# A decode-attention kernel: K loaded for four batches at once, and the engines' loops by fours of batches

## The chip, the cores and the metric

The kernel runs on one core of a Trainium2 chip. The metric is the device time of one execution in microseconds (us). Times below are medians. The profile is of one execution of each kernel. Its span, from the first to the last instruction, is about 1.7 to 2.1 us shorter than the time of the run (194.7 us for 196.53 before the change). Engines: PE is the matmul engine (PEld are its weight loads), DVE the vector engine, ACT the scalar engine, POOL the GpSimd engine, SP the sync engine, which here only issues DMAs.

## The reference

One query token per batch, grouped-query attention over the last 512 keys of a cache, with projections before and after:

```python
B, Sq, D = 32, 1, 512
Hq, Hkv, Sk, Dh = 32, 8, 2048, 128          # all bf16
W = min(4096, max(256, Sk // 4))            # 512
q = (x @ wq).reshape(B, Sq, Hq, Dh).transpose(0, 2, 1, 3)
k = repeat(k_cache[:, :, Sk - W:, :], 4, axis=1)
v = repeat(v_cache[:, :, Sk - W:, :], 4, axis=1)
p = softmax(einsum("bhqd,bhkd->bhqk", q, k) * Dh ** -0.5)
o = einsum("bhqk,bhkd->bhqd", p, v)
return o.transpose(0, 2, 1, 3).reshape(B, Sq, Hq * Dh) @ wo
```

The windows of K and V are 33.5 MB each, wq and wo 4 MB each: 75.5 MB to read, whatever the schedule.

## The kernel before

Per batch, K arrives in two DMAs of 512 KB with 4 KB rows (partition = key block and head). PE transposes it into PSUM, 32 transposes of 128x128 in four banks `KT_ps`. DVE copies three of the banks to `KT_sb`, ACT the fourth. Eight score matmuls per batch accumulate four batches in one PSUM tile `S_ps`. Softmax (maximum on DVE, exponential on ACT, four scaled writes into the block-diagonal `P_ex` on DVE), the transposes of P and their copies on ACT then go by four batches. PV goes by batch, and its result is copied out by DVE (`oT`).

The loops of the three engines are interleaved by batch:

```python
# SP: K runs LEAD = 5 batches ahead of V; rings of NK = 6 and NV = 8 batches
for b in range(B + LEAD):
    if b < B: load_k(b)
    if b >= LEAD: load_v(b - LEAD)
# PE, PVLAG = 6
for it in range(B + PVLAG):
    if it < B: transposes(it)
    if 1 <= it <= B: scores(it - 1)
    if it >= PVLAG: pv_matmuls(it - PVLAG)
    if it % 4 == 1 and 5 <= it <= B + 1: pt_transposes((it - 5) // 4)
    ...                                     # cut: selection of outputs, once, near the end
# DVE
for it in range(B + PVLAG + 1):
    if it < B: kt_evac(it, 0)
    if it >= PVLAG + 1: ot_evac(it - PVLAG - 1)
    ...                                     # cut
    if it % 4 == 1 and 5 <= it <= B + 1: softmax_b((it - 5) // 4)
    if it < B: kt_evac(it, 1); kt_evac(it, 2)
    if it % 4 == 0 and 4 <= it <= B: softmax_a((it - 4) // 4)
# softmax_b, the P_ex write: P_ex is [P, NR=16, NS=32, G4=4]
P_ex[rows, :, :, c], P_f32[rows, :].rearrange("p (r s) -> p r s", r=NR)
# the score operand: KT_sb is [P, NKT=3, 2, NR, G4, NS]
rhs = KT_sb[:, b % NKT, h, :, c, :]         # 16 runs of 32 elements
```

## Time and profile before

| | before |
|---|---|
| time | 196.4 us (3 runs, 196.2 to 196.75) |
| span of the profile | 194.7 us |
| PE, DVE, ACT busy | 74%, 52%, 30% of the span |
| DMA | 16 engines busy in nearly every slice, 405 to 412 GB/s in slices 4 to 38 |

The span of the kernel before in 40 equal slices; digits are tenths (9 is 90% or more), PEclk is the granted clock of PE, GB/s what the DMA engines moved:

```profile
PE   0448995877897679749777988779776978937881
...
PEclk9999999999699978996999699979998887975558
DMA  5999999999999999999999999999999999999960
GB/s 204 426 420 406 412 405 411 407 410 407 409 407 407 408 408 410 407 407 410 407 407 410 409 407 407 410 406 408 408 406 411 405 410 405 412 405 412 406 251 31
```

The DMA row is full from slice 2 to slice 38, and no other row is. The chain of waits that ended last, by engine and then by line (SPq is the DMA queue of SP; L144 issues V, L136 K), says the same:

```profile
SPq 68%; DMA 23%; PE 5%; issue 3%; DVEq 0%; DVE 0%
SPq L144 37%; SPq L136 26%; DMA K_sb<-in_k_cache_dram 15%; DMA w_sb<-in_wo_dram 8%; SPq L155 5%; PE KT_ps L243 4%; SPq L130 1%; PE S_ps L260 1%; PE QO_ps L293 0%; PE KT_ps L337 0%; SPq L118 0%; DVEq L47 0%; DVE out_sb L418 0%
```

The costliest groups (line, engine, operation, output and inputs, count, busy us and mean ns of one, then the idle time before them and its main cause):

```profile
L243 PE MATMUL KT_ps<-perm,K_sb 128*128 128x128 bf16 x1024 | 75.2, 235 | 22.4 <-DMA K_sb<-in_k_cache_dram 22.2
L361 DVE COPY KT_sb<-KT_ps 128x1024 bf16<-128x1024 bf16 x96 | 63.6, 689 | 52.2 <-PE KT_ps L243 52.0
...
L435 ACT ACTIVATE KT_sb<-KT_ps 128x1024 bf16<-128x1024 bf16 x32 | 32.8, 1023 | 82.3 <-PE KT_ps L243 82.3
...
L383 DVE TENSOR_SCALAR P_ex<-P_f,recip 32x512 bf16<-32x512 f32 x32 | 25.4, 793 | 1.2
L260 PE MATMUL S_ps<-KT_sb,QBD 128*32 128x512 bf16 x256 | 22.2, 428 | 0.0
```

And PE's wait for K (total us, times, longest):

```profile
PE KT_ps L243 <- DMA K_sb<-in_k_cache_dram: 22.2, 35, 1.3
```

PE waits for K 35 times, 22 us in all. So it has slack: with faster loads it could go faster. That slack is about 0.7 us (22.2 over 32 batches) in each 5.1 us.

### The profile page before, as it was taken

The numbers are of one execution on the slowest core, as the hardware profiler recorded it, in microseconds if no ns is written. First come the engines' busy times: TensorE is split into PE (matmuls) and PEld (weight loads), VectorE is DVE, ScalarE is ACT, GpSimd is POOL, SyncE is SP. The second block draws the span as 40 slices with busy tenths as digits, with TensorE's granted clock in tenths as the row PEclk, the third lists the DMA queues.
The fourth block names the chain that finished last, engine by engine and source line by source line (L and its number), as shares of the span: only waits on it lengthen the run. The fifth ranks groups of instructions, "written<-read, shape, count | busy, mean of one in ns | idle before, by whom it ended". The sixth has DMA issues, their size and how long they took to land.

```text
span 194.7 us, 6153 instructions
## 1 busy us (share of the span) xinstructions
PE 144.0 (74%) x2724; PEld 114.9 (59%) x2724; DVE 102.1 (52%) x190; ACT 57.6 (30%) x70; POOL 15.0 (8%) x45
## 2 busy tenths in 40 slices
PE   0448995877897679749777988779776978937881
PEld 0337773755586567537555667557666667636760
DVE  0005778745684459533944587447943574670211
ACT  3001535622262126213252236204420352213101
POOL 8502000000020001000000000000000000000000
PEclk9999999999699978996999699979998887975558
DMA  5999999999999999999999999999999999999960
GB/s 204 426 420 406 412 405 411 407 410 407 409 407 407 408 408 410 407 407 410 407 407 410 409 407 407 410 406 408 408 406 411 405 410 405 412 405 412 406 251 31
DMA packets 20282, 75.97 MB, mean 390 GB/s; under 512 B 2272, under 2 KB 2336, under 8 KB 19744
## 3 DMA queue, kind: packets, MB, share of 16 engines
q1 hardware_dynamic: 20208, 75.54, 97.2%
q8 instruction: 22, 0.36, 0.8%
q10 hardware_dynamic: 48, 0.03, 0.1%
q14 instruction: 4, 0.03, 0.0%
HBM read 75.53 MB, written 0.03 MB: 388 GB/s over the span
## 4 chain that ended last, share of the span: by engine, by line
SPq 68%; DMA 23%; PE 5%; issue 3%; DVEq 0%; DVE 0%
SPq L144 37%; SPq L136 26%; DMA K_sb<-in_k_cache_dram 15%; DMA w_sb<-in_wo_dram 8%; SPq L155 5%; PE KT_ps L243 4%; SPq L130 1%; PE S_ps L260 1%; PE QO_ps L293 0%; PE KT_ps L337 0%; SPq L118 0%; DVEq L47 0%; DVE out_sb L418 0%
## 5 line engine op out<-in xcount | busy, mean ns | idle before, releaser
L243 PE MATMUL KT_ps<-perm,K_sb 128*128 128x128 bf16 x1024 | 75.2, 235 | 22.4 <-DMA K_sb<-in_k_cache_dram 22.2
L361 DVE COPY KT_sb<-KT_ps 128x1024 bf16<-128x1024 bf16 x96 | 63.6, 689 | 52.2 <-PE KT_ps L243 52.0
L243 PEld LDWEIGHTS KT_ps<-perm,K_sb 128*128 128x128 bf16 x1024 | 65.6, 106 | 30.0 <-DMA K_sb<-in_k_cache_dram 28.4
L435 ACT ACTIVATE KT_sb<-KT_ps 128x1024 bf16<-128x1024 bf16 x32 | 32.8, 1023 | 82.3 <-PE KT_ps L243 82.3
L293 PEld LDWEIGHTS QO_ps<-PT_sb,V_sb 128*128 128x128 bf16 x1024 | 28.3, 97 | 17.8 <-issue 13.5
L293 PE MATMUL QO_ps<-PT_sb,V_sb 128*128 128x16 bf16 x1024 | 31.1, 171 | 3.3 <-DMA V_sb<-in_v_cache_dram 1.3
L383 DVE TENSOR_SCALAR P_ex<-P_f,recip 32x512 bf16<-32x512 f32 x32 | 25.4, 793 | 1.2
L260 PE MATMUL S_ps<-KT_sb,QBD 128*32 128x512 bf16 x256 | 22.2, 428 | 0.0
L453 ACT ACTIVATE PT_sb<-PT_ps 128x1024 bf16<-128x1024 bf16 x16 | 15.5, 1021 | 19.4 <-PE PT_ps L275 19.4
L203 POOL COPY QBD<-QT_sb 128x32 bf16<-128x32 bf16 x32 | 8.5, 279 | 116.1 <-PE S_ps L260 108.1
L275 PE MATMUL PT_ps<-ident,P_ex 128*128 128x128 bf16 x128 | 9.4, 231 | 9.8 <-DVE P_ex L383 9.8
L275 PEld LDWEIGHTS PT_ps<-ident,P_ex 128*128 128x128 bf16 x128 | 7.9, 104 | 10.9 <-DVE P_ex L383 10.8
L397 DVE CAST oT_sb<-QO_ps 128x32 bf16<-128x32 f32 x32 | 9.3, 289 | 7.5 <-PE QO_ps L293 7.5
L221 PE MATMUL PT_ps<-xT_sb,w_sb 128*128 128x32 bf16 x128 | 4.1, 188 | 6.4 <-DMA w_sb<-in_wq_dram 6.4
L367 DVE TENSOR_REDUCE maxv<-S_ps 128x1 f32<-128x512 f32 x8 | 5.5, 691 | 5.4 <-PE S_ps L260 5.4
L221 PEld LDWEIGHTS PT_ps<-xT_sb,w_sb 128*128 128x128 bf16 x128 | 3.7, 104 | 6.8 <-DMA w_sb<-in_wq_dram 4.6
L443 ACT ACTIVATE P_f<-S_ps,negmax 128x512 f32<-128x512 f32 x8 | 5.5, 687 | 6.3 <-DVE negmax L369 6.3
L260 PEld LDWEIGHTS S_ps<-KT_sb,QBD 128*32 128x32 bf16 x256 | 3.9, 96 | 3.9 <-issue 1.4
L353 DVE CAST QT_sb<-PT_ps 128x512 bf16<-128x512 f32 x1 | 0.7, 691 | 10.3 <-PE PT_ps L221 10.3
L337 PE MATMUL KT_ps<-w_sb,o_sel 128*32 128x128 bf16 x128 | 3.8, 289 | 1.9 <-DMA w_sb<-in_wo_dram 1.5
L337 PEld LDWEIGHTS KT_ps<-w_sb,o_sel 128*32 128x32 bf16 x128 | 2.9, 131 | 2.7 <-DMA w_sb<-in_wo_dram 2.2
L427 ACT ACTIVATE QT_sb<-PT_ps 128x512 bf16<-128x512 f32 x1 | 0.6, 597 | 12.0 <-PE PT_ps L221 12.0
(28 smaller groups left out, 22.4 us busy)
## 6 DMA issues: line engine op xcount, KB each, us to landing
K_sb<-in_k_cache_dram SPq DMA_DIRECT2D x64, 512.0 KB, 15.6
V_sb<-in_v_cache_dram SPq DMA_DIRECT2D x64, 512.0 KB, 15.4
w_sb<-in_wq_dram SPq DMA_DIRECT2D x4, 1024.0 KB, 8.3
w_sb<-in_wo_dram SPq DMA_DIRECT2D x8, 512.0 KB, 15.4
x_sb<-in_x_dram ACTq DMA_DIRECT2D x1, 32.0 KB, 2.9
out_dram<-out_sb SPq DMA_DIRECT2D x1, 32.0 KB, 1.5
```

The source lines that it names most:

```text
L136: sp.dma_start(K_sb[:, b % NK, h].rearrange("p r d -> p (r d)"), cache_rows(k_cache, b, h)).then_inc(sem_k[b % NK][h], 16)
L144: sp.dma_start(V_sb[:, b % NV, h].rearrange("p r d -> p (r d)"), cache_rows(v_cache, b, h)).then_inc(sem_v[b % NV], 16)
L155: sp.dma_start(wo_sb[:, hg].rearrange("p i n -> p (i n)"), wo[hg * 512:(hg + 1) * 512, :].rearrange("(m i) n -> m (i n)", i=4),).then_inc( ...
L243: ins = pe.matmul(KT_ps[:, t, i * 128:(i + 1) * 128], lhsT=K_sb[:, b % NK, h, 8 * (t % 2) + i, :], rhs=perm[:, :, :], start=True, stop=Tru ...
L260: ins = pe.matmul(S_ps[32 * c:32 * c + 32, :], lhsT=QBD[:, b % NQB, g, :], rhs=KT_sb[:, b % NKT, h, :, c, :], start=(j == 0 and h == 0), s ...
L275: ins = pe.matmul(PT_ps[:, r // 8, (r % 8) * 128:(r % 8 + 1) * 128], lhsT=P_ex[:, r, :, :].rearrange("p s g -> p (s g)"), rhs=ident[:, :], ...
L293: ins = pe.matmul(QO_ps[:, 16 * h:16 * h + 16], lhsT=V_sb[:, b % NV, h, r, :], rhs=PT_sb[:, q % 2, r, :].rearrange("p (c n) -> p c n", c=G ...
L361: dve.tensor_copy(KT_sb[:, b % NKT, t // 2, 8 * (t % 2):8 * (t % 2) + 8, :, :], KT_ps[:, t, :]).then_inc(dve_T, 1)
L383: dve.tensor_scalar(P_ex[rows, :, :, c], P_f32[rows, :].rearrange("p (r s) -> p r s", r=NR), recip[rows, q:q + 1], None, op0=ALU.mult,).th ...
L397: dve.tensor_copy(oT_sb[:, :, b], QO_ps[:, 0:HQ]).then_inc(dve_oT, 1)
L435: act.activation(KT_sb[:, b % NKT, 1, 8:16, :, :], KT_ps[:, 3, :], ACTF.Copy).then_inc(act_T, 1)
L453: act.activation(PT_sb[:, q % 2, 8 * i:8 * i + 8, :].rearrange("p r n -> p (r n)"), PT_ps[:, i, :], ACTF.Copy,).then_inc(act_PT, 1)
```

## The change

The intent is longer rows. K's partition becomes (batch, head) x 4 key blocks for four batches at once, so a row is 16 KB and a DMA 2 MB. One transpose now holds 32 (batch, head) pairs, so a score matmul over all 512 keys can start only when all 128 transposes of four batches are copied out. KT becomes one buffer of four batches, and everything goes by fours. Core of the diff:

```diff
-            for b in range(B + LEAD):
-                if b < B:
-                    load_k(b)
-                if b >= LEAD:
-                    load_v(b - LEAD)
+            def load_k(n):                       # 16 chunks of 2 MB, ring of 3
+                q, e = divmod(n, 2)
+                ...
+                rows = k_cache[4*q:4*q+4, :, SK-W:, :].rearrange("b g (s r) d -> (b g) s (r d)", s=KS)
+                sp.dma_start(K_sb[:, n % NK]..., rows[:, :, e*CR*DH:(e+1)*CR*DH])
+            for n in range(NCH):
+                load_k(n)
+                if n >= 2:
+                    load_v(2 * n - 4)
+                    load_v(2 * n - 3)
 ...
-        KT_sb = sb("KT_sb", [P, NKT, 2, NR, G4, NS], BF16)
+        KT_sb = sb("KT_sb", [P, KR, 4 * G, KS], BF16)      # KR = 128, KS = 4
-                        rhs=KT_sb[:, b % NKT, h, :, c, :],
+                            rhs=KT_sb[:, :, G * j + g, :],  # 128 runs of 4 elements
 ...
+            for q in range(NQUAD):               # PE
+                transposes(4 * q)
+                transposes(4 * q + 1)
+                if q >= 1:
+                    pt_transposes(q - 1)
+                    pv_matmuls(4 * q - 4)
+                    pv_matmuls(4 * q - 3)
+                transposes(4 * q + 2)
+                transposes(4 * q + 3)
+                scores(q)                        # 32 matmuls of 512 columns
+                if q >= 1:
+                    pv_matmuls(4 * q - 2)
+                    pv_matmuls(4 * q - 1)
 ...
-                        P_ex[rows, :, :, c], P_f32[rows, :].rearrange("p (r s) -> p r s", r=NR),
+                        P_ex[rows, :, :, c].rearrange("p r (s e) -> p e r s", e=NE),
+                        P_f32[rows, :].rearrange("p (e r s) -> p e r s", e=NE, r=NR),
 ...
+            for q in range(NQUAD):               # DVE
+                kt_evac(4 * q)
+                kt_evac(4 * q + 1)
+                if q >= 1:
+                    ot_evac(4 * q - 4)
+                    ot_evac(4 * q - 3)
+                kt_evac(4 * q + 2)
+                kt_evac(4 * q + 3)
+                softmax_a(q)
+                if q >= 1:
+                    ot_evac(4 * q - 2)
+                    ot_evac(4 * q - 1)
+                softmax_b(q)
```

## The prediction

> **What bounds the kernel now.** DMA. The 40-slice row shows the 16 DMA engines at 90% or more in slices 2 to 38 at 405-412 GB/s; the chain of waits is 68% the sync engine's queue (issues of about 1.08 us each[...]) and 23% DMA. PE is busy 74% of 194.7 us but has slack: its waits on K loads sum to 22.2 us, about 1 us per batch period of 5.1 us.
>
> **What the change does to DMA.** K rows grow from 4 KB to 16 KB. In the trace's packet records a 4 KB packet takes a median 161 ns and an 8 KB one (wq) 309 ns, so about 13 ns are fixed; a 16 KB packet should take about 605 ns instead of 4 x 161. K's 33.5 MB (82 us) should fall by 4 to 5 us; 20.2 thousand packets by about 6 thousand. [...] If DMA still bound, the time would be about 192 us.
>
> **What it does to the schedule.** PE's work is the same, but goes by fours: four batches of transposes, then 32 score matmuls, in one single-buffered KT tile. Overlap between neighbours becomes a serial loop. I walked the wait graph of both kernels with durations of the trace (timeline): 32 transposes 1.97 us, a KT copy 0.65 back to back on DVE and 1.0 on ACT, 8 score matmuls 0.61, maximum 0.69 + 0.15, exponential 0.69 + 0.19, four P_ex writes 3.3, P transposes 1.07, their two copies 1.94, PV 0.96 plus about 0.4 for the oT handshake. The walk of before gives score times within 2 us of the trace.
>
> For after it gives a PE loop of 21.5 us per four batches at full clock, against 19.5 us in which DMA brings four batches. Idle PE per loop: about 3 us while transposes wait for DVE, which must finish P_ex before it drains the next KT banks; 2.5 us in which PV waits for ACT's PT copies; 1.4 us in which scores wait for the last KT copy; 1.1 us oT handshakes. So K waits vanish and PE with its DVE/ACT handshakes becomes critical. First scores about 29.5 us, the eighth about 180, then 22 us of tail (softmax, PT, four PV, selection, output). Span about 204 us at full clock; at the 0.9 granted in the steady slices of before, about 210. The run time is 1.7 us over the span.
>
> The DMA gain is thus off the critical path: loads end earlier or stall on buffers, while PE ends later. A 2 MB first K load also delays the first transposes by about 3 us.
>
> Predicted: 210 us, range 200 to 224; faster 0.06, same 0.08, slower 0.86.
>
> **What would show it.** The chain: PE, DVE and ACT lines instead of the sync queue. Transposes wait on DVE copies rather than on K DMAs. Score start to score start about 21 to 23 us. wo lands well before its matmuls. DMA share falls late; K packets 16 KB near 605 ns.
>
> **What would make it wrong.** (a) The score operand now has 8-byte runs at a 256-byte stride (before 64-byte runs); if PE reads that at half speed, add some 12 us. (b) P_ex writes with stride 64 bytes innermost; if they take 1.1 us instead of 0.8, add about 7. (c) PE idle in lumps may lower the granted clock more. (d) If PE overlaps more than my walk says, DMA stays the bound and the time is 191 to 196. [...]

## The result, and the profile after

The changed kernel takes 248.37 us (4 runs, 247.65 to 249.5), the kernel before 196.33 us beside it. The ratio is 1.2654, 95% interval 1.2613 to 1.2695.

The predicted direction and mechanism show up at once; the size does not. The slices after:

```profile
PE   0418854697278765688269746679269737777365
...
PEclk9999995759975897769975997779875997689755
DMA  6999999999999994799839992998659999700000
```

The DMA row is no longer full, and it ends five slices early. The loads are done by about 216 us of 247. PEclk drops to 5 to 7 tenths in a repeating pattern. The chain is now PE with DVE and ACT (L239 transposes, L387 P_ex writes, L289 PV, L256 scores, L461 copies of the P transposes), and only 7% of it is DMA:

```profile
PE 53%; DVE 22%; ACT 11%; DMA 7%; issue 6%; SPq 1%; DVEq 0%; ACTq 0%
PE KT_ps L239 30%; DVE P_ex L387 14%; PE QO_ps L289 10%; PE S_ps L256 8%; DMA K_sb<-in_k_cache_dram 7%; ACT PT_sb L461 6%; ACT KT_sb L443 4%; DVE oT_sb L402 2%; DVE maxv L371 2%; PE PT_ps L271 2%; DVE KT_sb L365 2%; PE KT_ps L339 1%; DVE recip L379 1%; SPq L131 1%; DVE negmax L373 1%
```

The same groups as before:

```profile
L239 PE MATMUL KT_ps<-ident,K_sb 128*128 128x128 bf16 x1024 | 89.9, 272 | 39.8 <-DVE KT_sb L365 35.2
...
L365 DVE COPY KT_sb<-KT_ps 128x1024 bf16<-128x1024 bf16 x96 | 63.2, 689 | 22.4 <-PE KT_ps L239 22.1
L443 ACT ACTIVATE KT_sb<-KT_ps 128x1024 bf16<-128x1024 bf16 x32 | 32.7, 1023 | 128.9 <-PE KT_ps L239 128.9
...
L387 DVE TENSOR_SCALAR P_ex<-P_f,recip 32x512 bf16<-32x512 f32 x32 | 42.7, 1335 | 1.2
...
L256 PE MATMUL S_ps<-KT_sb,QBD 128*32 128x512 bf16 x256 | 19.7, 451 | 10.4 <-ACT KT_sb L443 10.4
```

The KT copies cost per instruction what they cost before, on DVE (689 ns) and on ACT (1023 ns). Three means have grown: the P_ex write from 793 to 1335 ns, the transposes from 235 to 272 ns, the score matmul from 428 to 451 ns. (The score group as a whole is busy less, 19.7 us in place of 22.2: in the kernel before, six of the 32 bursts of eight fell into stretches of half clock and took 1.02 to 1.04 us in place of 0.61.) PE's waits have changed kind. Two new ones, and the old one, which happens once, at the start:

```profile
PE KT_ps L239 <- DVE KT_sb L365: 35.2, 7, 6.3
...
PE QO_ps L289 <- ACT PT_sb L461: 15.5, 8, 2.1
...
PE KT_ps L239 <- DMA K_sb<-in_k_cache_dram: 4.7, 1, 4.7
```

And SP's own waits show that DMA is no longer in the way. It waits 129 us for K buffers to come free, and at the end 41 us with everything issued:

```profile
SPq L138 <- PE KT_ps L239: 129.1, 13, 17.5
SPq L164 <- ACT out_sb L483: 40.6, 1, 40.6
```

One loop of four batches, in order of time (start us, us, engine, line, operation, tiles, count, and in brackets the idle time before and what ended it):

```profile
111.67 2.47 PE L256 MATMUL S_ps<-KT_sb,QBD 128*32 128x512 bf16 x32 [1.32 <-ACT KT_sb L443]
...
114.06 0.96 PE L289 MATMUL QO_ps<-PT_sb,V_sb 128*128 128x16 bf16 x32
...
116.23 1.95 PE L239 MATMUL KT_ps<-ident,K_sb 128*128 128x128 bf16 x32
...
116.77 5.45 DVE L387 TENSOR_SCALAR P_ex<-P_f,recip 32x512 bf16<-32x512 f32 x4
...
123.00 3.47 PE L239 MATMUL KT_ps<-ident,K_sb 128*128 128x128 bf16 x32 [4.82 <-DVE KT_sb L365]
...
126.31 1.06 PE L271 MATMUL PT_ps<-ident,P_ex 128*128 128x128 bf16 x16
...
127.43 1.94 ACT L461 ACTIVATE PT_sb<-PT_ps 128x1024 bf16<-128x1024 bf16 x2
...
129.42 1.01 PE L289 MATMUL QO_ps<-PT_sb,V_sb 128*128 128x16 bf16 x32 [2.05 <-ACT PT_sb L461]
...
131.69 5.99 PE L239 MATMUL KT_ps<-ident,K_sb 128*128 128x128 bf16 x64
```

The loop is serial. Scores end at 114.1. Softmax runs until 122.2, of which 5.45 us are four P_ex writes. Only then does DVE copy the next KT banks, and PE, which has filled all four banks at 118.2, stands still for 4.8 us. The 32 transposes after it take 3.47 us, and the 64 at 131.69 take 5.99, where the 32 at 116.23 take 1.95. The next scores start at 138.99, 27.3 us after these. PE by stretch in the same loop (length, PE busy and count, granted clock, DMA share, GB/s) shows why:

```profile
118.20:123.00 4.80, 0.00 (x0) 0.98 0.89 359
123.00:126.30 3.30, 3.30 (x32) 0.51 0.02 6
129.40:131.70 2.30, 1.89 (x65) 0.55 0.97 413
131.70:135.20 3.50, 3.50 (x40) 0.50 0.97 404
```

After the idle stretch the granted clock is half, and again from 129.4 to 135. The clock records of this trace are 0.5 or 1.0, in stretches of 3.4, 6.8 or 13.7 us (17.2 us for the last). The half clock from 122.8 us follows the idle 4.8 us, the half clock from 129.6 us an idle stretch of only 2.05 us. From 123.0 to 126.2 us PE ran nothing but transposes, and from 126.2 us the clock was full. How long PE may idle before the clock falls is not shown: in the kernel before, no wait of PE between 40 and 150 us was longer than 1.35 us, and the clock was still at half for 3.4 us about every 20 us (mean 0.91 from 45 to 100 us).

### The profile page after: what moved, and what is told of

It is laid out like the page before. It is cut to its first block, busy times and chain, and to the rows that moved or that the text cites. A ratio compares the mean times of both kernels' runs of the same rounds, so it can differ in the third digit from the quotient of the medians. Undisturbed runs are those within 1.5% of the kernel's fastest.

```text
span 247.1 us, 5986 instructions
## 1 busy us (share of the span) xinstructions
PE 157.0 (64%) x2724; PEld 138.4 (56%) x2724; DVE 124.8 (51%) x190; ACT 56.9 (23%) x70; POOL 11.9 (5%) x43
## 4 chain that ended last, share of the span: by engine, by line
PE 53%; DVE 22%; ACT 11%; DMA 7%; issue 6%; SPq 1%; DVEq 0%; ACTq 0%
PE KT_ps L239 30%; DVE P_ex L387 14%; PE QO_ps L289 10%; PE S_ps L256 8%; DMA K_sb<-in_k_cache_dram 7%; ACT PT_sb L461 6%; ACT KT_sb L443 4%; DVE oT_sb L402 2%; DVE maxv L371 2%; PE PT_ps L271 2%; DVE KT_sb L365 2%; PE KT_ps L339 1%; DVE recip L379 1%; SPq L131 1%; DVE negmax L373 1%
## 5 line engine op out<-in xcount | busy, mean ns | idle before, releaser
L239 PE MATMUL KT_ps<-ident,K_sb 128*128 128x128 bf16 x1024 | 89.9, 272 | 39.8 <-DVE KT_sb L365 35.2
L239 PEld LDWEIGHTS KT_ps<-ident,K_sb 128*128 128x128 bf16 x1024 | 86.2, 127 | 41.7 <-DVE KT_sb L365 36.4
L443 ACT ACTIVATE KT_sb<-KT_ps 128x1024 bf16<-128x1024 bf16 x32 | 32.7, 1023 | 128.9 <-PE KT_ps L239 128.9
L289 PE MATMUL QO_ps<-PT_sb,V_sb 128*128 128x16 bf16 x1024 | 31.7, 172 | 22.1 <-ACT PT_sb L461 15.5
L289 PEld LDWEIGHTS QO_ps<-PT_sb,V_sb 128*128 128x128 bf16 x1024 | 28.7, 100 | 29.1 <-ACT PT_sb L461 16.9
L387 DVE TENSOR_SCALAR P_ex<-P_f,recip 32x512 bf16<-32x512 f32 x32 | 42.7, 1335 | 1.2
L256 PE MATMUL S_ps<-KT_sb,QBD 128*32 128x512 bf16 x256 | 19.7, 451 | 10.4 <-ACT KT_sb L443 10.4
L256 PEld LDWEIGHTS S_ps<-KT_sb,QBD 128*32 128x32 bf16 x256 | 7.4, 99 | 19.1 <-issue 17.6
L461 ACT ACTIVATE PT_sb<-PT_ps 128x1024 bf16<-128x1024 bf16 x16 | 15.5, 1024 | 3.9 <-PE PT_ps L271 3.9
L201 POOL COPY QBD<-QT_sb 128x32 bf16<-128x32 bf16 x32 | 6.0, 232 | 156.7 <-PE S_ps L256 148.2
(26 smaller groups left out, 19.7 us busy)
```

Source lines behind the costliest of these rows:

```text
L239: ins = pe.matmul(KT_ps[:, t, i * 128:(i + 1) * 128], lhsT=K_sb[:, n % NK, 32 * (v % 2) + 8 * t + i, :], rhs=ident[:, :], start=True, stop ...
L256: ins = pe.matmul(S_ps[32 * c:32 * c + 32, :], lhsT=QBD[:, (4 * q + j) % NQB, g, :], rhs=KT_sb[:, :, G * j + g, :], start=(j == 0 and h == ...
L289: ins = pe.matmul(QO_ps[:, 16 * h:16 * h + 16], lhsT=V_sb[:, b % NV, h, r, :], rhs=PT_sb[:, q % 2, r, :].rearrange("p (c n) -> p c n", c=G ...
L387: dve.tensor_scalar(P_ex[rows, :, :, c].rearrange("p r (s e) -> p e r s", e=NE), P_f32[rows, :].rearrange("p (e r s) -> p e r s", e=NE, r=NR),
L443: act.activation(KT_sb[:, r0:r0 + 8].rearrange("p r a s -> p (r a s)"), KT_ps[:, 3, :], ACTF.Copy).then_inc(act_T, 1)
L461: act.activation(PT_sb[:, q % 2, 8 * i:8 * i + 8, :].rearrange("p r n -> p (r n)"), PT_ps[:, i, :], ACTF.Copy,).then_inc(act_PT, 1)
```

## Experiments

The theory going in: the schedule by fours makes a PE loop with DVE and ACT handshakes, as predicted, and three terms of it were too small: the P_ex write, the clock, and the score burst. The rivals: the new K loads themselves hurt, or a wait that the walk of the prediction does not have. Each term was first taken away alone, then all three, then the two halves of the change (loads and schedule) were separated. Two kernels (e2, e4) and the combination e6 permute keys. Comparison is a weak test of key order here, and the other kernels' order rests on their index arithmetic as well.

### e1_pex_order: another walk over the same P_ex write

```diff
-                        P_ex[rows, :, :, c].rearrange("p r (s e) -> p e r s", e=NE),
-                        P_f32[rows, :].rearrange("p (e r s) -> p e r s", e=NE, r=NR),
+                        P_ex[rows, :, :, c].rearrange("p r (s e) -> p r s e", e=NE),
+                        P_f32[rows, :].rearrange("p (e r s) -> p r s e", e=NE, r=NR),
```

> The changed kernel, with the P_ex write walking its elements in another order (result unchanged): writes go with an 8-byte step in runs of 32 as before the change, reads of P_f with a 256-byte step. Theory W (the 64-byte-step writes made the write slow, 1335 ns against 793): one write falls to about 0.8 us, the loop of four batches from 27.3 to about 25.1 us, the run from 248 to about 231 us. Rival R (any walk that breaks up the contiguous read is as slow): still about 1.3 us a write, and 248 us.

Measured: 223.6 us (2 runs), ratio 1.139. The P_ex group of e1 (duration min/median/max):

```profile
L387 DVE TENSOR_SCALAR P_ex<-P_f,recip x32: 791/800/807, 34.3 to 204.8; 32x512 bf16<-32x512 f32 x32
```

The write is back at 0.80 us. The loop falls from 27.3 to 23.9 us, more than the 2.1 us of the four writes. The clock rose as well, from 0.818 to 0.861, with PE's idle stretch shorter (2.67 us in place of 4.82). Theory W holds: the step of the writes costs, not the step of the reads, which is 256 bytes here. The write took 0.80 us with an 8-byte step and 1.33 with a 64-byte step; the f32 reads with a 256-byte step cost DVE nothing visible (800 ns in the median, against 792 with the contiguous read of the kernel before).

### e2_pex_old: the old P_ex instruction, wrong result

```diff
-                        P_ex[rows, :, :, c].rearrange("p r (s e) -> p e r s", e=NE),
-                        P_f32[rows, :].rearrange("p (e r s) -> p e r s", e=NE, r=NR),
+                        P_ex[rows, :, :, c], P_f32[rows, :].rearrange("p (r s) -> p r s", r=NR),
```

> The changed kernel with the very P_ex instruction of the kernel before (contiguous read, 8-byte-step write). WRONG RESULT on purpose, the keys come out permuted; timing only. Expected of the write: 0.79 us. If the write sits on the serial loop, as the chain says, all of its 2.2 us per loop comes back: loop 25.1 us, run about 231 us. Rival (the write hides behind other waits): under 5 us gained.

Measured: 223.4 us (2 runs), loop 23.9 us. The same as e1 within noise. So the write is on the serial loop, and e1's order costs no more than the original. Both runs gained more than the 17 us expected, for the reason just given.

### e3_warm: PE kept active in its gaps

```diff
+            def dummies(dst, n):
+                for _ in range(n):
+                    pe.matmul(dst[:, 64:512], lhsT=ident[:, :], rhs=QT_sb[:, 0:14, :]..., ...)
                 transposes(4 * q)
+                if q >= 1:
+                    dummies(PT_ps[:, 1, :].bitcast(F32), 20)
                 transposes(4 * q + 1)
                 if q >= 1:
                     pt_transposes(q - 1)
+                    pe.wait_ge(dve_oT, 4 * q - 4)
+                    dummies(QO_ps, 8)
                     pv_matmuls(4 * q - 4)
 ...
+                if q >= 1:
+                    pe.wait_ge(act_exp, q)
+                    dummies(S_ps, 5)
                 scores(q)
```

> The changed kernel with dummy matmuls (448 columns, result unused) put where PE idles in the loop: 20 before the transposes that wait for DVE, 8 before PV waits for the PT copies, 5 before the scores. They remove no wait; they only keep PE active. Theory C (PE's lumps of idle time lower the granted clock, and 3 of 4 groups of 32 transposes then run at half clock, 3.5 and 5.9 us for 32 and 64 instead of 2 and 3.9): clock rises from 0.82 to over 0.95, the loop falls by about 3 us, the run to about 224 us. Rival (the clock is not on the critical path, or idle time doesn't set it): the run stays within 3 us of 248.

Measured: 227.3 us (2 runs), ratio 1.158, mean clock 0.955, loop 23.8 us. The clock row of e3:

```profile
PEclk9999999799999999969999999999999999999557
```

And its transposes, 229 ns in the mean in place of 272:

```profile
L239 PE MATMUL KT_ps<-ident,K_sb 128*128 128x128 bf16 x1024 | 67.9, 229 | 13.7 <-DVE KT_sb L380 8.9
```

The kernel does strictly more work and takes 21 us less. Theory C holds: with the lumps of idle time filled, the clock rose from 0.818 to 0.955, and the transposes, which had paid for the lower clock, took 67.9 us in all in place of 89.9.

### e4_score_runs: the old run length of the score operand, wrong result

```diff
+        KT_old = KT_sb[...].rearrange("p r a s -> p (r a s)").rearrange("p (n r c s) -> p n r c s", n=8, r=NR, c=G4)
-                            rhs=KT_sb[:, :, G * j + g, :],
+                            rhs=KT_old[:, 2 * j + h, :, c, :],
```

> The changed kernel, its 32 score matmuls of a loop reading KT as 16 runs of 32 elements (64 bytes) as in the kernel before, in place of 128 runs of 4 (8 bytes). WRONG RESULT on purpose (keys and heads come out mixed); timing only. If the short runs cost PE time: the burst falls from 2.48 us to about 1.9 us (four times the 0.61 us of before, less three pipeline ends) and the run by about 5 us, to 243. If the burst is slow for another reason (more matmuls in a row, weights loaded in between): 2.48 us and 248 us again.

Measured: 242.1 us (2 runs), ratio 1.233. The score matmul after the change, and in e4 (min/median/max):

```profile
L256 PE MATMUL S_ps<-KT_sb,QBD x256: 441/451/461, 29.9 to 222.9; 128*32 128x512 bf16 x128
```

```profile
L258 PE MATMUL S_ps<-KT_sb,QBD x256: 376/379/390, 29.8 to 215.3; 128*32 128x512 bf16 x128
```

Group e4 is busy 15.3 us in all, against 19.7: 1.91 us a burst in place of 2.47. So runs of 8 bytes read slower than runs of 64 by about 0.56 us per burst, or 29%.

### e6_all_three: all three sizes put back, wrong result

The diffs of e1, e3 (with 10 dummies in place of 20) and e4 together.

> The changed kernel with the three suspected sizes put back together: P_ex written in the order of e1, dummy matmuls as in e3 (10, 8, 5), score runs as in e4. WRONG RESULT on purpose because of the last. What stays is the schedule by fours alone, at nearly full clock. The prediction's walk gave a loop of 21.5 us and a span of 204 us for this: run 203 to 209 us. If something else in the changed kernel costs time (rival: a wait that the walk does not have), it stays above 212.

Measured: 205.8 us (2 runs), ratio 1.048, clock 0.95. Score start to score start is 21.06 us in four loops of seven, 21.6 in one and 22.7 in two, 21.6 in the mean; the walk gave 21.5. Part of one loop of PE:

```profile
83.41 2.26 PE L241 MATMUL KT_ps<-ident,K_sb 128*128 128x128 bf16 x32 [0.44 <-DVE KT_sb L382]
...
88.61 0.96 PE L299 MATMUL QO_ps<-PT_sb,V_sb 128*128 128x16 bf16 x32 [0.54 <-ACT PT_sb L478]
...
95.83 1.91 PE L266 MATMUL S_ps<-KT_sb,QBD 128*32 128x512 bf16 x32 [0.37 <-ACT KT_sb L460]
```

This is the loop that the prediction described, with the write and the clock at the speeds it assumed and the burst at 1.91 us (whether the walk took about that, or four times 0.61, 2.44 us, is not on record): span 205.1 us in the profiled run and 203.0 in the other, against the walk's 204. The rest of the changed kernel's loss, 42.6 us, is those three sizes. Taken alone they gave 24.8, 21.1 and 6.2 us, 52.1 in sum. They overlap, since a shorter wait also raised the clock (0.861 in e1).

### e11_after_4k: only the DMA half undone

```diff
-                sp.dma_start(K_sb[:, n % NK]..., rows[:, :, e * CR * DH:(e + 1) * CR * DH]
-                ).then_inc(sem_k[n % NK], 16)
+                for s4 in range(4):
+                    d0 = (e * CR + 16 * s4) * DH
+                    sp.dma_start(K_sb[:, n % NK, 16*s4:16*s4+16]..., rows[:, :, d0:d0 + 16 * DH]
+                    ).then_inc(sem_k[n % NK], 16)
 ...
-                        pe.wait_ge(sem_k[n % NK], 16 * (n // NK + 1))
+                        pe.wait_ge(sem_k[n % NK], 64 * (n // NK + 1))
```

> The changed kernel as it is, with each 2 MB K load cut into 4 DMAs of 512 KB with 4 KB rows: undoes the DMA half of the change and keeps the schedule by fours. If the loads have no part in the loss: 248 us again, within 2 us. If the 16 KB rows at a 512 KB pitch hurt: clearly below 248.

Measured: 248.4 us (2 runs). With 4 KB rows the changed kernel is just as slow. The row size has no part in the loss, and its gain is worth nothing here because DMA is off the critical path (7% of the changed kernel's chain).

### e5_pipe: the new loads with the old interleaving

The loads of the change; scores of a quarter of the keys (128 columns of `S_ps`, 32 matmuls) right after its transposes; KT in a ring of three quarters; the loops of PE, DVE and ACT as in the kernel before; P_ex as in e1.

```diff
-                scores(q)
+                for it in range(B + PVLAG):      # as before, it = one quarter of four batches
+                    if it < B: transposes(it)
+                    if 1 <= it <= B: scores(it - 1)
+                    if it >= PVLAG: pv_matmuls(it - PVLAG)
 ...
-                            S_ps[32 * c:32 * c + 32, :],
+                            S_ps[32 * c:32 * c + 32, 128 * w:128 * w + 128],
-                            rhs=KT_sb[:, :, G * j + g, :],
+                            rhs=KT_sb[:, v % NKT, :, G * j + g, :],
```

> K loaded as in the changed kernel (2 MB DMAs, 16 KB rows), but transposes, scores and PV interleaved as in the kernel before: the scores of each quarter of the keys right after its transposes (32 matmuls of 128 columns in place of 8 of 512), KT in a ring of three quarters, softmax pieces between KT copies; P_ex write order of e1. Theory S (the loss is the schedule by fours and nothing in the K loads): DMA bounds again, 16 KB packets of about 611 ns against four of 161 ns, run 190 to 193 us, faster than the kernel before by 2 to 3%. Rival D (the 16 KB rows[...] hurt the loads): slower than 197 us with the DMA share still full.

Measured: 199.5 us (4 runs, 198.3 to 200.5), ratio 1.014. The old interleaving, with the P_ex order of e1, brings back 49 of the 52 us lost (in the schedule by fours, e1's order alone brought back 24.8; the interleaving without it was not run). The number is the one that D gave, over 197 us with the DMA row at 9 up to slice 37, but D's cause is not there: the loads were not hurt, as the 16 KB packets took 614 ns in the median, against about 161 for each of four 4 KB packets before. That is within 2% of what the fixed and the per-byte part of the smaller packets give (605, from 161 ns for 4 KB and 309 for 8 KB). S was not met either: the loads ended about 3 us earlier (the last of V landed at 178.0 us in place of 181.5, the last of wo at 189.0 in place of 191.6; the expectation of e7 says 5), but PE's tail ended late:

```profile
180.27 1.89 PE L274 MATMUL PT_ps<-ident,P_ex 128*128 128x128 bf16 x16 [2.97 <-DVE P_ex L382]
...
184.27 3.15 PE L304 MATMUL KT_ps<-oT_sb,band 128*128 128x224 bf16 x16
...
192.47 3.60 PE L336 MATMUL KT_ps<-w_sb,o_sel 128*32 128x128 bf16 x128 [0.38 <-DVE o_sel L415]
```

The selection (L304, 3.15 us; its 16 matmuls took 1.69 us in e1) sits between two PV steps, and the last 128 matmuls (L336) start only at 192.5, with wo already loaded.

### e7_pipe_tail and e8_pipe_4k: the tail mended, then 4 KB rows again

e7 is e5 with K loaded one chunk earlier relative to V, and the selection moved into the wait for the last softmax. e8 is e7 with the cut of e11.

```diff
-    NK = 3
-    NV = 8
+    NK = 4
+    NV = 7
 ...
-                if n >= 2:
-                    load_v(2 * n - 4)
-                    load_v(2 * n - 3)
+                if n >= 3:
+                    load_v(2 * n - 6)
+                    load_v(2 * n - 5)
 ...
-                if it == SELCUT + PVLAG:         # after pt_transposes
+                if it == SELCUT + PVLAG - 1:     # before pt_transposes
                     select(0, nb, ...)
 ...
```

> e5 with its tail mended: the K ring has 4 chunks and V 7 batches, so that each K chunk is loaded 2 MB (about 5 us) earlier relative to V, and the selection of the first 28 batches runs while the last softmax is under way. In e5 the loads ended about 5 us earlier than before, but PE's tail ended late. Theory T (e5 lost to its tail alone): run 190 to 194 us, faster than the kernel before. Rival (the coarse 2 MB loads stall PE or V throughout): 197 us or more.

> e7, with each 2 MB K load cut into 4 DMAs of 512 KB with 4 KB rows, the same bytes to the same places. Undoes only the row size. If the 16 KB packet is what K gains (611 ns against 4 x 161): 4 to 5 us slower than e7. If the row size is worth nothing: the same as e7 within 1 us.

Measured: e7 196.05 us (4 runs), ratio 0.999, interval 0.996 to 1.002: no different from the kernel before. e8 197.97 us, ratio 1.009. Theory T is half right: the tail and the longer lead of K together were worth 3.4 us (they were not tried apart), but PE kept the loop at the loads' pace (its chain is 64% PE). The row size is worth 1.9 us of the 4 to 5 expected, which fits a kernel that DMA does not bind.

### e9_pipe_act and e10_pipe_act_4k: half of the P_ex writes on ACT

```diff
-                for c in range(G4):                     # DVE
+                for c in range(2):
 ...
+            def p_ex(q):                                # ACT
+                ...
+                for c in range(2, 4):
+                    act.activation(P_ex[rows, :, :, c]..., P_f32[rows, :]..., ACTF.Copy, scale=recip[rows, q:q + 1])
```

> e7 with half of the P_ex writes (two of four per loop) given to ACT, which is busy 30% of the time: DVE is then kept from its KT copies for about 1.7 us in place of 3.4 per four batches. In e7 the chain of waits was 64% PE and only 8% DMA, with score starts 19.1 us apart per four batches, so PE with its waits still bound it narrowly. Theory P (that wait for DVE is what keeps e7 from the loads' own end): 191 to 193.5 us, 1.5 to 3% faster than the kernel before. Rival (PE is bound by its own work, instruction supply and clock): within 1 us of e7, 196.

> e9, with each 2 MB K load cut into 4 DMAs of 512 KB with 4 KB rows. If e9 is bound by the loads, this shows the row size's worth undiluted: 4 to 5 us slower than e9, 196 to 197 us. If e9 is still bound by PE: within 2 us of e9, as e8 was of e7.

Measured: e9 196.4 us, ratio 0.998; e10 197.8 us, ratio 1.007. Theory P fell: freeing DVE gained nothing. e10 is 1.3 us slower than e9, which by its expectation means that PE still bounds e9. The rival of P is what the chain of e9 shows, with DVE gone from it and "issue" (time in which the engine waited for nothing that the profile shows) at 16%:

```profile
PE 61%; issue 16%; DVE 2%; ACT 2%; DVEq 0%; ACTq 0%
```

In PE's timeline of e9 such stops come every 6 to 7 us, in the middle of a group, whichever group it is:

```profile
65.73 0.61 PE L294 MATMUL QO_ps<-PT_sb,V_sb 128*128 128x16 bf16 x18 [1.25 <-issue]
...
72.20 1.78 PE L242 MATMUL KT_ps<-ident,K_sb 128*128 128x128 bf16 x20 [1.79 <-issue]
...
78.94 0.59 PE L260 MATMUL S_ps<-KT_sb,QBD 128*32 128x128 bf16 x22 [0.71 <-issue]
...
85.44 0.32 PE L260 MATMUL S_ps<-KT_sb,QBD 128*32 128x128 bf16 x8 [1.34 <-issue]
```

That is every 126 matmuls with their weight loads between the stops shown. The guess at the cause is the queue of instruction loads (packets, MB, share of the engines):

```profile
q8 instruction: 27, 0.44, 0.9%
```

PE alone has 3492 matmuls here, the kernel before has 2724 (its own queue shows 22 packets). In the packet records these are blocks of 16 KB that take about 1.08 us each, and every stop of this kind of over 1 us in e9 begins 0.3 to 1.3 us after one of them starts, and ends 1 to 2 us after it has landed. It is a coincidence in time; no run took the instruction loads away, and that the blocks cause the stops was not shown. The counts of the other traces agree with the guess. Between 25 and 180 us, PE has 20 such stops of over 0.6 us in e9 (28.9 us in all), 12 in e7 (17.1) and 7 in e5 (13.4), all with 3492 matmuls; it has 1 in e12 (2980 matmuls) and none in the kernel before, in the changed one, in e3 or in e6 (2724 to 2955). The blocks load no faster in the kernel before (1.08 us), so a block in flight is not enough by itself. The stops may also be a part of what e5 and e7 lacked, beside the tail. (On ACT one P_ex write took 1.46 us, on DVE 0.81, so that e9 also made one side of the softmax longer.)

### e12_chunk: fewer PE instructions

e9 with scores of a whole chunk in two bursts of 16 matmuls of 256 columns (512 fewer matmuls), KT in a ring of two chunks, V in a ring of 6, three P_ex writes on DVE and one on ACT.

```diff
-            def scores(v):
-                q, w = divmod(v, 4)
+            def scores(n, half):
+                q, w = divmod(n, 2)
 ...
-                for j in range(4):
+                for j in (2 * half, 2 * half + 1):
 ...
-                            S_ps[32 * c:32 * c + 32, 128 * w:128 * w + 128],
+                            S_ps[32 * c:32 * c + 32, 256 * w:256 * w + 256],
```

> e9 with fewer PE instructions: the scores of a whole K chunk (64 of its key rows, 256 columns) in two bursts of 16 matmuls, in place of 32 matmuls of 128 columns per quarter (512 fewer matmuls in all); KT in a ring of two chunks, V ring of 6; three of four P_ex writes on DVE, one on ACT. In e9 PE stood idle 1.3 to 2.2 us about every 130 matmuls with nothing to wait for in the profile (issue, 15.6% of the chain)[...]. Theory I (instruction count and PE work bound e9): issue idle falls by a quarter or more, DMA or PE at DMA's pace, run 190 to 194.5 us. Rival (the coarse loads or the tail bound it): within 1 us of 196.

Measured: 193.0 us (5 runs, 192.9 to 193.2), ratio 0.983, interval 0.981 to 0.984. This beats both kernels, by 1.7% over the one before: clear of noise. The chain and slices of e12:

```profile
DMA 33%; PE 22%; SPq 17%; DVE 5%; issue 2%; ACT 1%; DVEq 0%
```

```profile
PEclk9999999969999999699999589999697599978555
DMA  5999999999999999999999999999999999999960
```

DMA is first in the chain again and its row is full to the end; "issue" is 2% of the chain. Its last matmuls wait for wo, which landed at 188.1 us; in e9 all of wo had landed, at 189.1, before PE came to the first of them. Theory I gave the right number. Several things changed at once between e9 and e12 (instruction count, PE time of the scores, the rings of KT and V, the split of P_ex), so that instruction count alone did it is argued, not shown. Nor was e12 run with 4 KB rows.

## Why the prediction was right and wrong

- **Bound by DMA before, and K packets get cheaper: right.** The 16 KB packet takes 611 to 615 ns in the median against the estimated 605. Over all K packets and 16 engines, 2048 x 617 ns in e12 come to 79.0 us, against 8192 x 163 ns, 83.6 us, before: 4.6 us. In the changed kernel itself the mean was 660 ns, 84.5 us in all, since 150 of its 2048 packets took over 1.3 times the median. Its twin with 4 KB rows, e11, has 726 packets as slow as that, where the kernel before has 50. So they come with the schedule and not with the rows; what slows them is not shown.
- **The gain lies off the critical path, PE with DVE and ACT takes over: right.** The chain went from 68% SP queue to 53% PE, 22% DVE and 11% ACT. PE waited for K once, at the start. wo had long landed when its matmuls came. e11 shows that the loads have no part in the time; e5 shows that the old interleaving, with the P_ex order of e1, brings nearly all of it back.
- **"A PE loop of 21.5 us per four batches at full clock": the step that failed, by two of its terms.** It measured 27.3. The waits were the right ones: for DVE about 3 us was predicted and 5.0 measured (35.2 over 7 loops), for ACT's PT copies 2.5 and 1.9, for the last KT copy 1.4 and 1.3. But two sizes that were carried over from the trace of before did not carry over, and they make 2.15 and 3.5 of the 5.8 us:
  - "four P_ex writes 3.3" measured 5.45. The new access pattern has a 64-byte step. Risk (b) named it, at 1.1 us a write and 7 us in all, an estimate. It was 1.33 us, 17 us for 32 writes, and 25 us with the clock that it pulls down (e1).
  - "at the 0.9 granted in the steady slices of before" measured 0.818, and the half clock fell on the transposes, the largest group: 3.5 us for 32 in place of 1.95. Risk (c) named it without a size. It was 21 us, 3.5 us a loop (e3).
- **The score burst is not shown to be mis-sized.** "8 score matmuls 0.61", four times over, is 2.44 us, and the burst measured 2.47. The 1.9 us, with three pipeline ends taken off, is an expectation of e4, made after the result. What e4 does show is the price of the 8-byte runs: risk (a) gave 12 us for half speed, an assumption; it was 6 us.
- **The walk itself: right.** With the three sizes put back (e6) it gives span and loop within 1 or 2%: 203 to 205 us against 204, 21.1 us in most loops and 21.6 in the mean against 21.5. The first scores start at 30.4 us and the eighth at 181.7, against 29.5 and 180. Half a microsecond a loop of this agreement hangs on what the walk took for the burst.
- **"A 2 MB first K load also delays the first transposes by about 3 us": 4.3 us** (start at 19.2 in place of 14.9 us).
- The range ended at 224 us. Over 210 that has room for risk (a) or risk (b) at the sizes given, but not for both (229), and hardly any for (c). All three came true, (a) at half its size, and two of them feed each other: with the longer write PE's idle stretch was 4.82 us and the clock 0.818, with the shorter one 2.67 us and 0.861 (e1).

## What to carry to other kernels

A load can be made cheaper and be worth nothing if the schedule that comes with it makes the stages behind it work in larger lumps (here 248.4 us with the long rows as without them, e11). The layout did not force that here (e5): check first whether the engines that share buffers can still be interleaved. When a layout changes, durations of instructions whose access patterns change must not be carried over from the old trace (the P_ex write went from 793 to 1335 ns), nor the clock of a matmul engine whose waits become lumpy (0.818 here, where 0.9 was carried over, and 0.955 with the waits filled, e3). Here a kernel with the long rows came out ahead, by 1.7%, only after the old interleaving had been restored and the number of matmuls kept down. That the rows are what these 1.7% consist of fits their packets (4.6 us less) but was not shown; where the rows alone were undone, they were worth 1.9 us (e7 and e8) and 1.3 us (e9 and e10).
